# A delta-rule attention feeding an FFN: another layout of the opening, and the input weights' low halves by identity products in PSUM

## The chip, the cores and the metric

One core of one Trainium2 chip. The metric is the device time of one execution in microseconds, median of several runs.

## What is computed

The first part is a linear attention with the delta rule, over 4 batches, 8 heads, 768 positions and a head size of 48. Its output, 3072 tokens of 384 numbers, goes through an FFN with 2048 hidden units:

```python
k_n = k / (np.linalg.norm(k, axis=-1, keepdims=True) + 1e-06)
for t in range(S):
    y[:, :, t] = einsum('bhd,bhde->bhe', q[:, :, t], state)
    v_old = einsum('bhde,bhd->bhe', state, k_n[:, :, t])
    state = state + beta[:, :, t, None] * einsum('bhd,bhe->bhde', k_n[:, :, t], v[:, :, t] - v_old)
x = y.transpose(0, 2, 1, 3).reshape(B * S, H * D)
h = x @ w_in                                    # 384 x 2048
sp = np.maximum(h, 0.0) + np.log1p(np.exp(-np.abs(h)))
out = (h * erf(sp)) @ w_out                     # 2048 x 384
```

q, k, v and beta are f32; the two weight matrices arrive in float64.

## The kernel before

**The attention** is done in 12 chunks of 64 positions; 16 pairs of (batch, head) lie side by side, two heads in the two halves of the partitions. Two chunks make a solve group. For each chunk, TensorE multiplies the keys with themselves (`gram_mm` with "pg", line 259) and the keys with the queries ("pq", the same line); each of these comes in two halves of 16 pairs. `gram_a` (line 269) scales the first on VectorE into A. `gram_p` and `gram_p2` bring the second, masked, into qp, on top of the loaded rows of q. A goes to DRAM and comes back in blocks of 32 (`to_dram`, `to_blocks`); a triangular solve of 31 steps, each a multiply and an add (lines 320 and 322), inverts the blocks in the tile xb, on VectorE for group 0 and on GpSimd for the others; xb goes to DRAM (`put_blocks`, line 327) and from there into xm and A2 (`from_blocks`, `from_blocks2`). The merge (`merge_t` to `merge_m2`: a transposition on VectorE at line 349, products pe, pz and pm at lines 357, 370 and 383) joins the blocks. After it the chain has four steps j per chunk, one per batch: `chain_u`, `chain_s` and `chain_y` (lines 418, 431, 445) with copies between them; step j needs the state that step j - 4 left.

**The FFN** takes four steps j as a group of 256 tokens, 12 groups in all. `x_all` finds the largest magnitude by a product with the identity (`spread`, line 480), `x_tr` transposes, and x is split into two f16 halves xh and xl. The hidden layer has 16 ff tiles of 128 units; two of them make a unit with one PSUM tile ph. `ffn1` (line 622) is nine f16 products per tile: w_in's high half with xh and xl, its low half with xh. `e_sp` (softplus, ScalarE, line 644), `e_erf` (line 649), `e_mul` (line 653, VectorE), `e_split` (a cast to f16, line 660) and `e_rest` (line 666) give two f16 halves of the hidden layer, and `ffn2` (lines 677 to 679) sums their products with w_out in PSUM. Softplus and erf need different tables of ScalarE (line 139).

**The weights** come as pairs of 32-bit words, 12 loads of 512 KB for each matrix (`w_load`, line 490, into raw_in and raw_out). Each load is turned into f32 by `w_mask` (ScalarE, line 496), `w_sign` (VectorE, 503) and `w_bits` twice (VectorE, 509 and 511); `w_sum` (ScalarE, 516) takes the sum of magnitudes. After the last load `w_max`, `w_all` and `w_scale` give one scale per matrix. For each of the 16 ff tiles, `w_hi` (ScalarE, line 550) writes the f16 high half and `w_lo` (VectorE, line 559) the low half, scale x a - h. The f32 tile a lies in the same memory as the halves, one tile further on: the halves of tile i stand where a of tile i - 1 was. The scratch tiles of `early` lie in w_out's memory, so w_out's first loads come late.

**The order** of everything is written by hand. `on(t, fn)` puts down a step with a time; the list is sorted by it and then permuted by the table ORDER (line 33); each engine runs its instructions in that order. `us(x)` turns a time in microseconds into the unit of the table. All DMAs are issued on SyncE's queue, at most eight open at once. `fill` (line 157) puts a dummy matmul on zeros (line 154) on TensorE.

Of the kernel before, what the change touches and what calls it, by code (L numbers as in the profile page):

```python
# [82 lines left out]
@with_exitstack
def delta_ffn_kernel(ctx, tc, kT, qT, ktok, vtok, btok, w_in, w_out, cst, out):
# [151 lines left out]
    def norm_ops(sg, i, w=0):  # L236
        if i == 0:
            no[sg, w] = norms(sg, w)
        for fn in no[sg, w][i:i + 1] if sg < NSP else no[sg, w][3 * i:3 * i + 3]:
            fn()  # L240

    def load_kf(c, name):
        if c == 3 and name == "kpg":
            kf = early(5120, 1024).rearrange("p (a x) -> p a x", a=BP)
        else:
            kf = io.tile([P, BP, C], F32, tag="kf", bufs=3, name=f"{name}{c}")
# [49 lines left out]
    def to_blocks(c):  # L296
        sg, i = divmod(c, 2)
        if i == 0:
            gb_t[sg] = at.tile([P, 32, 32], F32, tag="gb", name=f"gb{sg}") if sg else early(0, 1024).rearrange("p (a b) -> p a b", a=32)
        dv = st[c]["d1"].rearrange("(f s) h a t -> f (h a) s t", f=2)  # L300
        for f in range(2):
            q0 = i * 64 + f * 32
            sp.dma_start(gb_t[sg][q0:q0 + 32], dv[f, :, :, f * 32:f * 32 + 32])

    def solve_init(sg):
        xb_t[sg] = at.tile([P, 32, 32], F32, tag="xb", name=f"xb{sg}") if sg else early(1024, 1024).rearrange("p (a b) -> p a b", a=32)
        x = xb_t[sg].rearrange("p a b -> p (a b)")
        ge.memset(x, 0.0)
        ge.memset(x[:, ::33], 1.0)
# [188 lines left out]
    def w_sign(nm, i):  # L498
        hi = wt[nm]["raw", i][:, :, 1]
        if i in (SGI if nm == "in" else SGO):  # L500
            ge.tensor_scalar(hi, hi.bitcast(F32), 0.0, -2.0 ** 31, op0=ALU.is_lt, op1=ALU.mult)
        else:
            ve.tensor_scalar(hi, hi, -0x80000000, None, op0=ALU.bitwise_and)
# [49 lines left out]

    def w_lo(nm, i, m):
        a, h, l = w_parts(nm, i)
        if m:
# [393 lines left out]
```

## Time and profile before

| | us |
|---|---|
| median of 3 runs | 709.91 |
| lowest and highest | 708.35, 712.67 |
| the profiled execution | 712.84 |
| its span in the trace | 711.1 |

The mean granted clock of TensorE in the profiled execution is 0.966 of 2.4 GHz. All rows further below are from this one execution; times in the trace count from the start of its span. The first product of an FFN group is the mark for how far the attention's opening reaches: group 0 starts at 138.99 us, and everything after it can be read as a second part of the program, in which the chain of the later chunks runs beside the FFN.

### The profile page before, as it was taken

Reading aid. Unit: us, or ns where it says so; the run is one execution under the profiler, and the core shown is the slowest. Engines: PE = TensorE matmul, PEld = TensorE weight load, DVE = VectorE, ACT = ScalarE, POOL = GpSimd, SP = SyncE. Lnnn points to the kernel's source line nnn. Section 1 sums busy time; section 2 is a strip of 40 time slices with the busy share of each in tenths; the row PEclk is TensorE's granted clock in tenths of the full one; section 3 lists DMA queues with packets and bytes.
Section 4 is the critical chain, followed back from the end, with each engine's and each line's share of the span. In section 5 each row is a group of like instructions: output and inputs, shape, how many; then the busy total and the mean of one; then the engine's idle time right before and its main releaser. Section 6 shows DMA issues by size and latency. Waiting matters only on the chain.

```text
span 711.1 us, 22264 instructions
## 1 busy us (share of the span) xinstructions
PE 669.8 (94%) x9475; PEld 507.0 (71%) x9475; DVE 435.9 (61%) x1000; ACT 543.4 (76%) x767; POOL 332.3 (47%) x500
## 2 busy tenths in 40 slices
PE   7999997468999999999999999999999999999997
PEld 5666675356777787886878777877868777777764
DVE  3699859367896874777745659564564455534321
ACT  6214374378899999995994986967978969879993
POOL 4403999344201797898139751178831223201111
PEclk9999997577999999999999999999999999999999
DMA  9486541770004615713445114432041120000000
GB/s 244 105 257 209 166 126 42 210 173 14 3 2 109 152 38 120 159 42 93 85 91 135 35 33 96 101 81 64 18 97 29 26 63 7 24 1 13 12 23 22
DMA packets 87395, 59.05 MB, mean 83 GB/s; under 512 B 67776, under 2 KB 77120, under 8 KB 87296
## 3 DMA queue, kind: packets, MB, share of 16 engines
q1 hardware_dynamic: 87296, 57.63, 32.8%
q8 instruction: 74, 1.21, 0.7%
q14 instruction: 25, 0.20, 0.1%
HBM read 43.45 MB, written 14.16 MB: 81 GB/s over the span
## 4 chain that ended last, share of the span: by engine, by line
PE 67%; ACT 13%; DVE 5%; DMA 5%; issue 4%; POOL 3%; SPq 1%; POOLq 0%; ACTq 0%; DVEq 0%
PE ph L622 18%; PE warm L154 10%; ACT L139 7%; PE pr L677 6%; PE pr L679 6%; PE pr L678 6%; PE pg L259 3%; PE pc L445 3%; PE pc L418 3%; PE pq L259 2%; PE pm L383 2%; DMA k<-ktok 2%; PE pc L431 2%; ACT L L649 2%; ACT L L644 2%
## 5 line engine op out<-in xcount | busy, mean ns | idle before, releaser
L139 ACT ACT_TABLE_LOAD x185 | 237.4, 1283 | 4.0 <-PEq L943 0.7
L622 PE MATMUL ph<-xh,w_in 128*128 128x256 f16 x1152 | 204.2, 274 | 4.2 <-DVE L L653 3.9
L622 PEld LDWEIGHTS <-w_in 128*128 128x128 f16 x1728 | 165.9, 98 | 32.3 <-DVE L L653 4.4
L666 POOL TENSOR_TENSOR H<-L,H 128x512 f16<-128x512 f32 x58 | 67.0, 1157 | 242.9 <-DVE H L662 154.9
L622 PE MATMUL ph<-xl,w_in 128*128 128x256 f16 x576 | 157.4, 273 | 0.0
L653 DVE SCALAR_TENSOR_TENSOR L<-ph,L 128x512 f32<-128x512 f32 x96 | 66.1, 689 | 114.4 <-ACT L L649 107.6
L677 PE MATMUL pr<-w_out,H 128*128 128x384 f16 x384 | 126.0, 328 | 0.0
L679 PE MATMUL pr<-w_out,H 128*128 128x384 f16 x384 | 125.6, 327 | 0.0
L678 PE MATMUL pr<-w_out,H 128*128 128x384 f16 x384 | 125.6, 327 | 0.0
L320 POOL TENSOR_TENSOR tmptmpg<-gb,xb 128x31 f32<-128x31 f32 (+15 forms) x155 | 88.8, 573 | 51.1 <-DMA gb<-d 42.0
L322 POOL TENSOR_TENSOR xb<-xb,tmptmpg 128x31 f32<-128x31 f32 (+15 forms) x155 | 88.6, 571 | 12.1
L644 ACT ACTIVATE L<-ph,xct 128x512 f32<-128x512 f32 x96 | 65.8, 687 | 21.6 <-POOL z L405 9.1
L154 PE MATMUL warm<-zero 128*128 128x384 f16 x455 | 80.2, 337 | 1.1 <-DVE zero L145 1.1
L405 POOL TENSOR_TENSOR z<-v,nm 64x192 f32<-64x192 f32 x96 | 58.5, 609 | 28.8 <-DMA v<-vtok 22.0
L154 PEld LDWEIGHTS <-zero 128*128 128x128 f16 x455 | 44.6, 100 | 31.8 <-issue 3.6
L649 ACT ACTIVATE L<-L 128x512 f32<-128x512 f32 x96 | 60.4, 629 | 1.1
L679 PEld LDWEIGHTS <-H 128*128 128x128 f16 x384 | 37.7, 98 | 25.1 <-issue 0.3
L677 PEld LDWEIGHTS <-H 128*128 128x128 f16 x384 | 37.6, 98 | 20.8 <-issue 0.2
L678 PEld LDWEIGHTS <-H 128*128 128x128 f16 x384 | 37.7, 98 | 18.6 <-issue 0.2
L666 DVE TENSOR_TENSOR H<-L,H 128x512 f16<-128x512 f32 x38 | 28.1, 740 | 25.9 <-ACT H L660 25.8
L424 DVE TENSOR_TENSOR z<-pc,ga 64x192 f32<-64x192 f32 x88 | 31.2, 355 | 17.7 <-PE pc L418 15.3
L259 PE MATMUL pq<-qp,kpq 48*64 48x64 f32 x640 | 25.4, 238 | 16.8 <-DMA qp<-qT 16.8
(138 smaller groups left out, 961.6 us busy)
## 6 DMA issues: line engine op xcount, KB each, us to landing
raw_in<-w_in SPq DMA_DIRECT2D x12, 512.0 KB, 7.6
raw_out<-w_out SPq DMA_DIRECT2D x12, 512.0 KB, 4.8
d<-A SPq DMA_DIRECT2D x20, 256.0 KB, 3.1
k<-ktok SPq DMA_DIRECT2D x12, 384.0 KB, 4.0
qp<-qT SPq DMA_DIRECT2D x24, 192.0 KB, 3.5
v<-vtok SPq DMA_DIRECT2D x48, 96.0 KB, 2.9
out<-ob SPq DMA_DIRECT2D x48, 96.0 KB, 2.2
kpg<-kT SPq DMA_DIRECT2D x22, 192.0 KB, 5.0
```

The source lines that it names most:

```text
L139: se.add_instruction(mybir.InstLoadActFuncSet(name=nc.get_next_instruction_name(), act_func_set_id=i, ins=[], outs=[]))
L154: te.matmul(wp[0], zero[:, :P], zero, start=True, stop=True)
L320: eng.tensor_tensor(tv, G[:, s, s + 1:].unsqueeze(1).broadcast_to([P, ncol, nr]), Xv[:, :, s:s + 1].broadcast_to([P, ncol, nr]), op=ALU.mult)
L322: eng.tensor_tensor(Xv[:, :, s + 1:], Xv[:, :, s + 1:], tv, op=ALU.add)
L622: te.matmul(ph, w[:, i, kt * P:kt * P + P], G[x][:, :, ksl], start=(m == 0), stop=(m == 8))
L644: se.activation(unit(g, u), G["ph", u], AF.Softplus, bias=0.0, scale=G["ct"])
L649: se.activation(Lu, Lu, AF.Erf, bias=0.0, scale=1.0)
L653: ve.scalar_tensor_tensor(Lu, fg[g]["ph", u], HSC, Lu, op0=ALU.mult, op1=ALU.mult)
L666: (ve if u % (2 if g < GLE else GLM) == 0 else ge).tensor_tensor(G["gl", u], unit(g, u), G["gh", u], op=ALU.subtract)
L677: te.matmul(G["po"][a], gh[:, o, asl], wout_h[:, i, :], start=(i == 0), stop=False)
L678: te.matmul(G["po"][a], gh[:, o, asl], wout_l[:, i, :], start=False, stop=False)
L679: te.matmul(G["po"][a], gl[:, o, asl], wout_h[:, i, :], start=False, stop=(i == NFF - 1))
```

## The change

Three things change.

First, the opening has a new layout. w_in's loads 0 to 5 come ahead, w_out's loads get times of their own (WOT), the solves of groups 0 and 1 are moved later in the table, the loads of chunks 2 and 3, of q and of the later kT come later, gram of chunks 2 and 3 is at 63 to 65 us of the table instead of 12 to 16, and v is loaded and scaled earlier for the first six steps. There are 390 fillers, spaced wider, instead of 440. The scratch tiles of `early` for chunk 3, gb and xb of group 0 and A of chunk 3 become tiles of their own. The table ORDER is a new one.

Second, w_in's low halves are made otherwise. TensorE multiplies a with a diagonal of the scale in f32 (`w_lo1`), adds the product of the f16 high half with minus the identity in the same PSUM bank, and ScalarE copies the sum as f16 (`w_lo2`). The banks are pr 0 to 2, in turn. w_out's low halves stay on VectorE.

Third, some steps change engines: for chunks 0 and 1 the mask of pq is multiplied on VectorE straight from PSUM (CP), half of the merge's copies of these chunks (CM) and the state's copy of steps 0 to 3 (S2A) are VectorE's, and the casts of groups 0 and 1 are all ScalarE's (8 more than before).

```diff
-C2 = 2.0
-C3 = 11.5
+C2 = 12.0
+C3 = 16.0
-WU = 440
-MT = 54
+WU = 390
+MT = 58
-WL = (1, 25, 25.1, 25.2, 25.3, 25.4, 25.5, 25.6, 26, 26.1, 26.2, 26.3)
+WL = (0.9, 0.95, 1.0, 1.05, 1.1, 1.15, 24, 24.1, 31.0, 32.5, 34.0, 35.5)
...
-WO = -4.1
+WOT = (36, 38, 40, 42, 76, 78, 62, 86, 88, 90, 72, 74)
+LPE = ("in",)
...
-S2A = (0, 1, 2, 3)
-CP = (0, 1, 2, 3)
-CM = (0,1,2,3)
+S2A = ()
+CP = (2, 3)
+CM = (2, 3)
...
+    def w_ident():
+        ve.tensor_scalar(idn, ident, -1.0, None, op0=ALU.mult)
+
+    def w_idsc(nm):
+        ve.tensor_scalar(ids[nm], ident, wt[nm]["sc"], None, op0=ALU.mult)
+
+    idn = con.tile([P, P], F16, name="idn")
+    ids = {nm: con.tile([P, P], F32, name=f"ids_{nm}") for nm in LPE}
+
+    def w_lo1(nm, i):
+        a, h, _ = w_parts(nm, i)
+        ps = wt[nm]["ps", i] = pr[i % PB][:, :DM]
+        te.matmul(ps, ids[nm], a, start=True, stop=False)
+        te.matmul(ps, idn, h, start=False, stop=True)
+
+    def w_lo2(nm, i):
+        se.copy(w_parts(nm, i)[2], wt[nm]["ps", i])
...
-        if (g * NFF // EU + u) % 8 in SPA:
+        if g < 2 or u in SPA:
             se.copy(G["gh", u], unit(g, u))
...
-    solve_end = [us(42), S1] + [chain_at(2 * sg * B) - MD - 1.3 for sg in range(2, NSG)]
-    solve_start = [us(22), us(30), SS2] + [solve_end[sg - 1] + 1.3 for sg in range(3, NSG)]
+    solve_end = [us(50), us(116)] + [chain_at(2 * sg * B) - MD - 1.3 for sg in range(2, NSG)]
+    solve_start = [us(28), us(76), SS2] + [solve_end[sg - 1] + 1.3 for sg in range(3, NSG)]
...
     for i in range(WU):
-        on(us(6 + 0.12 * i), fill)
+        on(us(6 + 0.17 * i), fill)
...
     for c in range(4):
-        t = (5.5, 8, 12.2, 15)[c]
-        ta = (10.6, 12, 16.3, 18)[c]
+        t = (5.5, 8, 63.2, 65.2)[c]
+        ta = (10.6, 12, 64, 66)[c]
...
-            on(ti, w_hi, nm, i, m)
-            on(ti + 0.2, w_lo, nm, i, m)
+            on(us(76.7 + 0.9 * i) if nm in LPE else ti, w_hi, nm, i, m)
+            if nm in LPE:
+                if i == 0:
+                    on(t + 0.18, w_idsc, nm)
+                tl = us(77 + 0.9 * i)
+                on(tl, w_lo1, nm, i)
+                on(tl + 0.05, w_lo2, nm, i)
+            else:
+                on(ti + 0.2, w_lo, nm, i, m)
```

Three places of the new order. The first is SyncE's queue around the solve of group 1, whose result is written to DRAM at line 327 (323 after the change) from xb into d_2 and d_3. Before, the loads of qp for chunk 2 come behind it:

```order
L398 DMA v_1484<-vtok 128x192
L327 DMA d_2_1684<-xb_163 64x1024
L327 DMA d_3_1694<-xb_163 64x1024
L490 DMA raw_out_1696<-w_out 128x1024
L334 DMA A_2_1700<-d_2_570 32x16x32 x2
L189 DMA qp_0_86<-qT 48x1024
L189 DMA qp_1_87<-qT 48x1024
```

After the change (lines of the new kernel, four less from 189 on):

```order
L245 DMA kpg_1749<-kT 48x1024 x2
L188 DMA qp_0_88<-qT 48x1024
L188 DMA qp_1_89<-qT 48x1024
L290 DMA d_4_2225<-A_2136 64x1024 x2
L323 DMA d_2_2282<-xb_1023 64x1024
L323 DMA d_3_2288<-xb_1023 64x1024
L394 DMA v_2297<-vtok 128x192
L299 DMA gb_2311<-d_4_2225 32x32x32 x2
```

These loads of qp are already those of chunk 3 (qp_0_88 and qp_1_89), which stood 24 rows behind xb's two rows before. Those of chunk 2 (qp_0_86 and qp_1_87) now stand 14 rows further up. So both pairs have moved from behind xb's way to DRAM to ahead of it.

The second is ScalarE around the first input products (softplus at line 644, 655 after; `w_hi` at line 550, 543 after). Before:

```order
L139 ACT_TABLE_LOAD
L644 ACTIVATE L_0_1879<-ph_0_1831,xct_1638 128x512
L550 ACTIVATE w_in<-w_in,sc_in 128x384
L496 ACTIVATE w_out<-raw_out_1799 128x512
L496 ACTIVATE w_out<-raw_out_1803 128x512
L362 COPY T_1841<-pe_1913 32x512 x2
L550 ACTIVATE w_in<-w_in,sc_in 128x384
```

After:

```order
L138 ACT_TABLE_LOAD
L655 ACTIVATE L_0_1789<-ph_0_1759,xct_1487 128x512
L563 CAST w_in<-pr_81 128x384
L543 ACTIVATE w_in<-w_in,sc_in 128x384
L655 ACTIVATE L_0_1789<-ph_1_1793,xct_1487 128x512
L138 ACT_TABLE_LOAD
L509 ACTIVATE raw_out_1541,mx_out<-w_out 128x512
L563 CAST w_in<-pr_82 128x384
L543 ACTIVATE w_in<-w_in,sc_in 128x384
```

Each high half now stands right behind the copy of the low half of the tile before it.

The third is TensorE ahead of the merge (pe at line 357, 353 after). Before, dummies stand on both sides of the first pe:

```order
L154 LDWEIGHTS zero
L154 MATMUL warm<-zero 128x384
L357 MATMUL pe_1083<-T_1067,A_0_656 32x32 x32
L154 LDWEIGHTS zero
L154 MATMUL warm<-zero 128x384
```

After, the last dummy is followed by the half gram of chunk 2, the product that `w_all` needs, and the two pe, and no dummy comes behind them:

```order
L153 LDWEIGHTS zero
L153 MATMUL warm<-zero 128x384
L255 MATMUL pg_1_1052<-kpg_518 64x64 x16
L476 MATMUL spin<-ident,m_in 128x128
L353 MATMUL pe_1088<-T_1073,A_0_546 32x32 x32
L353 MATMUL pe_1134<-w_out 32x32 x32
```

Ahead of the first pe TensorE runs 373 dummies and 12 half grams before, 405 and 10 after; behind it 82 dummies before, none after.

## Rows read from the trace of the kernel before

**Rows 1.** The page: busy times; the chain by line; one group (busy, mean ns).

```profile
PE 669.8 (94%) x9475; PEld 507.0 (71%) x9475; DVE 435.9 (61%) x1000; ACT 543.4 (76%) x767; POOL 332.3 (47%) x500
...
PE ph L622 18%; PE warm L154 10%; ACT L139 7%; PE pr L677 6%; PE pr L679 6%; PE pr L678 6%; PE pg L259 3%; PE pc L445 3%; PE pc L418 3%; PE pq L259 2%; PE pm L383 2%; DMA k<-ktok 2%; PE pc L431 2%; ACT L L649 2%; ACT L L644 2%
...
L139 ACT ACT_TABLE_LOAD x185 | 237.4, 1283 | 4.0 <-PEq L943 0.7
```

**Rows 2.** Chain that ended last, 30 to 140 us: start us, us, what.

```profile
33.54 3.88 PE pg L259 x128
37.42 46.58 PE warm L154 x286
...
126.19 0.45 SPq L327
...
127.38 6.33 DMA raw_out<-w_out
```

**Rows 3.** Waits (total us, times, longest): 110-160; SyncE queue 110-160; TensorE 139-181.

```profile
PE pq L259 <- DMA qp<-qT: 16.8, 3, 10.6
DVE w_in L559 <- ACT w_in L550: 15.0, 5, 10.1
...
SPq L327 <- POOL xb L322: 17.0, 1, 17.0
...
PE pq L259 <- DMA qp<-qT: 6.2, 2, 5.6
```

**Rows 4.** Timeline of SyncE's queue, 105 to 131 us.

```profile
126.19 1.09 SPq L327 DMA_DIRECT2D d<-xb  x2
...
129.72 0.90 SPq L189 DMA_DIRECT2D qp<-qT  x2
```

**Rows 5.** Timeline of TensorE, 125 to 142 us: start us, us, what, idle before it.

```profile
134.94 4.12 PE L259 MATMUL pq<-qp,kpq 48*64 48x64 f32 x64 [10.59 <-DMA qp<-qT]
138.99 0.40 PE L622 MATMUL ph<-xh,w_in 128*128 128x256 f16 x1
```

**Rows 6.** Stretches: busy time of each engine, granted clock, DMA share, GB/s.

```profile
core 0: us, PE busy (x) PEld busy (x) DVE busy (x) ACT busy (x) POOL busy (x), PEclk, DMA share, GB/s
...
117.70:139.00 21.30, 9.16 (x121) 7.65 (x121) 9.76 (x30) 7.04 (x16) 9.22 (x19) 0.50 0.52 134
139.00:162.00 23.00, 15.92 (x338) 14.01 (x339) 16.45 (x30) 17.63 (x33) 12.08 (x14) 0.74 0.73 173
162.00:181.00 19.00, 15.71 (x231) 12.16 (x227) 14.07 (x38) 15.70 (x30) 6.68 (x7) 0.82 0.05 13
181.00:209.00 28.00, 27.72 (x442) 21.64 (x442) 25.41 (x71) 27.16 (x47) 4.88 (x6) 1.00 0.01 2
...
630.00:690.00 60.00, 58.89 (x502) 43.45 (x500) 20.83 (x46) 59.17 (x72) 10.39 (x9) 1.00 0.06 14
```

**Rows 7.** Single lines: duration ns min/median/max, first and last start, forms.

```profile
L269 DVE TENSOR_TENSOR A<-pg,gn x20: 670/682/694, 21.0 to 454.7; 128x512 f32<-128x512 f32 x20
...
L349 DVE STREAM_TRANSPOSE T<-xm x22: 687/701/703, 75.9 to 567.9; 32x512 f32<-32x512 f32 x22
...
L480 PE MATMUL sp<-ident,xm x24: 272/275/376, 116.3 to 656.3; 128*128 128x128 f32 x24
...
L687 ACT ACTIVATE ob<-pr,xco x12: 572/583/588, 235.7 to 705.4; 128x384 f32<-128x384 f32 x12
...
L550 ACT ACTIVATE w_in<-w_in,sc_in x16: 597/612/617, 118.5 to 181.8; 128x384 f16<-128x384 f32 x16
...
L559 DVE SCALAR_TENSOR_TENSOR w_in<-w_in,sc_in x16: 606/619/965, 120.0 to 182.9; 128x384 f16<-128x384 f32 x16
```

**Rows 8.** Stretches of one us around 117, columns as in rows 6.

```profile
115.00:116.00 1.00, 0.70 (x22) 0.55 (x16) 0.97 (x5) 0.82 (x3) 0.92 (x2) 1.00 0.00 0
116.00:117.00 1.00, 0.68 (x4) 0.52 (x4) 1.00 (x3) 0.14 (x1) 0.93 (x3) 1.00 0.00 0
117.00:118.00 1.00, 0.27 (x1) 0.24 (x2) 0.90 (x4) 0.00 (x0) 0.92 (x2) 0.50 0.00 0
```

More of the change, by code (lines that the diff above doesn't have):

```diff
@@ L192, in norm_sq @@
         s = st[c]
-        if c < 4:
+        if c < 2:
             s["sq"] = ff.tile([P, BP, D], F32, tag="L", bufs=LB, name=f"sq{c}")
@@ L238, in norm_ops @@
             no[sg, w] = norms(sg, w)
-        for fn in no[sg, w][i:i + 1] if sg < NSP else no[sg, w][3 * i:3 * i + 3]:
+        for fn in no[sg, w][3 * i:3 * i + 3]:
             fn()
     def load_kf(c, name):
[L243 to L246, printed above, removed]
+        kf = io.tile([P, BP, C], F32, tag="kf", bufs=3, name=f"{name}{c}")
         st[c][name] = kf
@@ L263, in gram_a @@
         if i == 0:
-            if c in (1, 3):
-                s["A"] = early(1024 * (1 + (c + 1) // 2), 1024).rearrange("p (a x) -> p a x", a=BP)
+            if c == 1:
+                s["A"] = early(2048, 1024).rearrange("p (a x) -> p a x", a=BP)
             else:
@@ L298, in to_blocks @@
         if i == 0:
-            gb_t[sg] = at.tile([P, 32, 32], F32, tag="gb", name=f"gb{sg}") if sg else early(0, 1024).rearrange("p (a b) -> p a b", a=32)
+            gb_t[sg] = at.tile([P, 32, 32], F32, tag="gb", name=f"gb{sg}")
         dv = st[c]["d1"].rearrange("(f s) h a t -> f (h a) s t", f=2)
@@ L305, in solve_init @@
     def solve_init(sg):
-        xb_t[sg] = at.tile([P, 32, 32], F32, tag="xb", name=f"xb{sg}") if sg else early(1024, 1024).rearrange("p (a b) -> p a b", a=32)
+        xb_t[sg] = at.tile([P, 32, 32], F32, tag="xb", name=f"xb{sg}")
         x = xb_t[sg].rearrange("p a b -> p (a b)")
@@ L499, in w_sign @@
         hi = wt[nm]["raw", i][:, :, 1]
[L500 to L503, printed above, removed]
+        ve.tensor_scalar(hi, hi, -0x80000000, None, op0=ALU.bitwise_and)
     def w_bits(nm, i, k):
@@ L736, in delta_ffn_kernel @@
     for i in range(WU):
-        on(us(6 + 0.12 * i), fill)
+        on(us(6 + 0.17 * i), fill)
     on(us(0), clear_q)
-    for i, (fn, *a) in enumerate(((load_step, 0), (load_step, 1), (load_beta, 0), (load_kf, 0, "kpg"), (load_kf, 1, "kpg"), (load_q, 0), (load_q, 1),
+    for i, (fn, *a) in enumerate(((load_step, 0), (load_step, 1), (load_beta, 0), (load_kf, 0, "kpg"), (load_kf, 1, "kpg"),
                                   (load_cst,))):
@@ L742, in delta_ffn_kernel @@
     on(us(6.5), clear_x)
+    on(us(19), load_q, 0)
+    on(us(21), load_q, 1)
+    on(us(30), w_ident)
     for sg in range(2):
-        t = (4, 10.5)[sg]
+        t = (4, 20)[sg]
         if sg:
             for i, (fn, a) in enumerate(((load_step, 2), (load_step, 3), (load_beta, 1))):
-                on(us(0.6 + 0.05 * i), fn, a)
+                on(us(14 + 0.05 * i), fn, a)
         for x in range(2):
@@ L763, in delta_ffn_kernel @@
             on(us(ta + 0.6 * i), gram_a, c, i)
-        on(us((11.9, 13.3, 17.6, 19.3)[c]), to_dram, c)
+        on(us((11.9, 13.3, 66, 68)[c]), to_dram, c)
     on(us(14), to_blocks, 0)
@@ L767, in delta_ffn_kernel @@
     on(us(1), solve_init, 0)
-    on(us(0.8), load_kf, 2, "kpg")
-    on(us(0.85), load_kf, 3, "kpg")
+    on(us(30), load_kf, 2, "kpg")
+    on(us(30.5), load_kf, 3, "kpg")
     for c in range(2):
         for i in range(2):
-            t = 20.8 + 2.5 * (2 * c + i)
+            t = (56, 57, 71.5, 73)[2 * c + i]
             on(us(t), gram_mm, c, i, "pq")
-            on(us(t + 2.6), gram_p, c, i)
-            on(us(24.6 + 2.5 * (2 * c + i)), gram_p2, c, i)
+            on(us((64, 65, 72.7, 74.2)[2 * c + i]), gram_p, c, i)
     for sg in range(NSG):
@@ L809, in delta_ffn_kernel @@
             tm = [us(MT + x + 1.25 * c) for x in (0, 1.2, 2.2, 3.6, 4.8, 6, 7.2, 7.3, 8.5)]
-            on(us(22 + c), from_blocks, c)
-            on(us(42.4 + 0.2 * c), from_blocks2, c)
+            on(us(30 + c), from_blocks, c)
+            on(us(50.4 + 0.2 * c), from_blocks2, c)
             if c == 1:
@@ L828, in delta_ffn_kernel @@
         d = 1.0 if j >= 2 * B else 2.6 / SW / CS
-        on(t - 3.3 if j >= 2 * B else t - us(4) + us(0), load_v, j)
-        on(t - 1.2 if j >= 2 * B else t - us(2) + us(0), put_v, j)
+        on(t - 3.3 if j >= 2 * B else us(32 + 2 * j) if j < 6 else t - us(6) + us(0), load_v, j)
+        on(t - 1.2 if j >= 2 * B else us(52 + 1.3 * j) if j < 6 else t - us(2) + us(0), put_v, j)
         on(t, chain_u, j)
@@ L848, in delta_ffn_kernel @@
     for i in range(NRW):
-        t = WO + WD * i
+        t = us(WOT[i])
         on(t - 0.9, w_load, "out", w_out.bitcast(I32), i, RO[i])
@@ L855, in delta_ffn_kernel @@
         on(t + 0.5, w_sum, "out", i)
-    for nm, t in (("in", us(WI[-1] + 3)), ("out", WO + WD * (NRW - 1) + 1.2)):
+    for nm, t in (("in", us(WI[-1] + 3)), ("out", us(max(WOT)) + 1.2)):
         on(t, w_max, nm)
```

12 lines of the change are left out of this document (5 added, 7 removed).

## The prediction

> **What bounds the kernel now.** I read the page first. TensorE is busy 94% of the span, ScalarE 76%, VectorE 61% [rows 1]: a transfer or a VectorE step matters only where TensorE waits for it. A tenth of the chain that ended last is the dummy matmuls of line 154 [rows 1], so the opening is not bound by useful work of TensorE. The chain of waits then says by what. Dummy matmuls stand on it to 84.0 us; from 126.19 it runs through SyncE's queue, and a load of w_out that lands at 133.7 holds ScalarE [rows 2]. So there are two things to look at: where the opening ends, and a hole near 125 us.
>
> The lists of waits give the hole its size. TensorE waited 10.6 us in one piece for qp, VectorE 10.1 us for a high half of w_in, and SyncE stood 17.0 us at line 327 until GpSimd had finished xb [rows 3]. The queue's timeline shows how they hang together: line 327 goes at 126.19, and the loads of qp, which depend on nothing in the solve, stand behind it and go at 129.72 [rows 4]. TensorE starts pq at 134.94 and the first input product of the FFN at 138.99 [rows 5].
>
> The stretches of time give the cost around it. From 117.7 to 139 TensorE is busy 9.16 of 21.3 us, all at the 1.2 GHz level (granted 0.50). In the next two stretches it has 0.74 and 0.82, and is busy 15.92 of 23 and 15.71 of 19. From 181 on it is at 2.4 GHz and nearly full; ScalarE is busy 27.16 of 28 at first, and 59.17 of 60 at the end [rows 6]. What is won before 181 is therefore kept, unless the same stretch costs more elsewhere.
>
> **The end of the opening.** Before, TensorE ran 373 dummy matmuls and 12 half-chunk products of line 259 ahead of the first pe at 84.0. Now it runs 405 and 10. A dummy costs 46.58 / 286 = 0.163 us and a product of 32 matmuls 3.88 / 4 = 0.97 [rows 2]: 32 x 0.163 - 2 x 0.97 = +3.3 us at most, less some idle time in the first 37 us that the new order fills. The last of these products ends at 84 to 87; the mask of it (0.68) and a pair of transposes (1.4) stand behind it on VectorE [rows 7], so pe comes at 86 to 89. I take 87, 3 us late. The solve of group 0 costs nothing here: moved later, it still ends some 10 us ahead of the last dummy.
>
> After pe there were 82 more dummies in the gaps of merge and chain, 13.4 us of TensorE; now there are none. They did not delay what counts, since they filled gaps left by VectorE and GpSimd, and I take the same 33.7 us from pe to the end of the second chunk's chain: 117.7 + 3 = 120.7. The cover that goes with them is the clock's, a rival below. The solve of group 1 starts later too; it ended at 126.19 before and, by its place behind the last gram, may end 30 us later. Its result is wanted by chunk 2, whose tokens are the third group of the FFN, two groups behind the stretch spoken of here: I charge nothing.
>
> **The hole.** In the new queue the loads of qp for chunk 2, and for chunk 3 too, stand ahead of line 323 with xb. TensorE's 10.6 us for qp and VectorE's 10.1 us are gone [rows 3]; the rest of 117.7 to 139, 21.3 - 10.6 = 10.7 us, stays, with pq at 4.1 us [rows 5] if the clock is low and half of that if not. First input product: 120.7 + 10.7 = 131.4. What is late next is w_in's halves, below.
>
> **The low halves.** For 16 ff tiles one VectorE instruction of 0.62 us goes [rows 7], 9.9 us on an engine that is busy 61%: worth nothing by itself. In its place:
> - TensorE: one product of 384 f32 columns and one of 384 f16 columns per tile. The second has a row, 0.163. The first has none. From below it is that of an f16 product, 0.163; from above three f32 products of 128 columns, 3 x 0.275 = 0.83 [rows 7], which is the nearest row in type. Ends 0.33 and 0.99 per tile; I take 0.85, near the upper end, less a little because the records overlap. 16 x 0.85 = 13.6 us, between 5 and 16. Six of them stand ahead of the first input product, in a chain where TensorE has idle time; there I charge 2 of 5.1 us. Ten stand between the input products of the first group, 8.5 us.
> - ScalarE: a copy 128x384 from PSUM, 0.583 by the row of ob, 0.61 by that of the high half [rows 7]. 16 x 0.6 = 9.6 us, of which ten copies, 6.0 us, lie in the first two groups. There, 8 more casts of 0.61 come too (4.9). Against it, three high halves (1.8), two table loads of 1.283 [rows 1] and nine smaller instructions, which I estimate at half a us each, have moved ahead or gone, some 9 us. ScalarE's sum over the two groups grows by about 2 us; since it was idle for 9.5 of those 70 us [rows 6], I charge 1.
> - The hand-off. The halves of tile i overwrite the staging of tile i-1, so ScalarE's next high half waits for TensorE's product, and TensorE for the high half. Each round is 0.61 + 0.85 + 0.6 and some semaphores, 2.1 us, when nothing lies between; ten rounds are 21 us. Before, a round over VectorE was 0.61 + 0.62. From 139 to 181 TensorE stood idle for 10.4 of 42 us and VectorE for 11.5 (busy 16.45 and 14.07) [rows 6]: the ten rounds fit beside the chain in those 42 us, but TensorE's idle time there does not go.
>
> First input product: 131.4 + 2 = 133. From there the kernel took 711.1 - 139.0 = 572 us. Added: 8.5 (low halves) and 1 (ScalarE). Gained: between 139 and 181 TensorE waited for qp a second time, 5.6 us in one piece [rows 3]; that is chunk 3's, now also loaded ahead. Of the 7.0 us that the low clock cost there, 15.92 x 0.26 + 15.71 x 0.18 [rows 6], I credit 2, since the low halves' own products fill some of the gaps. 572 + 9.5 - 7.6 = 574, and the span is 133 + 574 = 707. The profiled execution took 712.84 beside its span of 711.1, and the median of the runs is 709.91, so 707 in the profile is 707 + 1.7 - 2.9 = 706 in the median. That is 0.6% under before; about 1% is what a measurement of this kernel can tell from no change.
>
> Everything else is worth little here: masks of the first chunks on VectorE instead of ScalarE and GpSimd (about 0.7 us each, off the chain), the earlier loads of w_in and v, which take from the same queue as before, and the pieces of staging that no longer live in w_out.
>
> **Rivals.**
> (a) The hand-offs are hidden and the clock stays up: faster by over 1%. pe comes at 86 (1 less), pq runs at 2.4 GHz (2 less) and the first six low halves cost half (1 less): first input product at 129. The other ten are nearer their lower bound (4.5 less), and 3.5 instead of 2 of the 7.0 us come back: the rest takes 568. Span 697, median 696. For it: the queue no longer has the cause of the hole in it. Against it: the granted clock was lost at 117 after two us in which TensorE was busy 70 and 68% [rows 8], with fillers not far ahead of it; the new order has none there.
> (b) The clock falls in the merge and stays down through the hand-offs: slower. Its place is 87 to 165 us. The price: some 10 us of TensorE work of the chain run at half speed, of which half shows (+5), and the six early low halves cost 2 more: first input product at 140. In the ten rounds behind it each low half takes 1.7 instead of 0.85 us, in a loop that ScalarE waits for (+8): the rest takes 582. Span 722, median 721. It decides once more than about 12 us are lost this way. For it: [rows 8], and 82 dummies gone. Against it: the low clock already covers 117 to 139 and parts of 139 to 181 in the kernel before [rows 6], so only the difference counts.
> The Trainium skill, in "TensorE: Matmul & The Clock Gate", section "HAM oscillation — how this bites in real kernels", says that bursts of matmuls with waits between them send the clock down each time, so that a kernel pays for gaps twice. By that rule the hand-off stretch would run at 1.2 GHz from end to end, and the time is that of (b). The trace agrees in part: from 139 to 181, with gaps, the granted clock is 0.74 and 0.82, neither 0.50 nor 1.00.
> (c) The hole only moves: the loads of qp come early, but the solve of group 1, which starts later now, holds the queue at line 323 longer, and TensorE or ScalarE stands there for a load behind it, v or k, for some 9 of the 10.6 us. Then 706 + 9 = 715, within 1%. For it: SyncE stood 17.0 us at that line before [rows 3]. Against it: what the first two groups of the FFN need stands ahead of it in the new queue.
>
> **How the numbers follow.** The forecast and its neighbours get 0.45, (a) 0.25, (b) 0.20, (c) 0.10. The forecast's own range is 700 to 714, and it lies over the 1% line (702.8) with a fifth to a quarter of its chance. Faster by over 1%: 0.25 + 0.10 = 0.35. Slower by over 1% (716.9): all of (b) and a little of (c), 0.22. Within 1%: 0.43. The range for 8 in 10 runs from the middle of (a), 694, to (b), 721.
>
> **What would show it.** Right: no wait of TensorE for qp over 3 us before the first input product; that product at 131 to 135; VectorE no longer among the waits of w_in; ScalarE waiting for the products of lines 559 and 560 in rounds of about 2 us; the f32 product at 0.6 to 0.83 us of TensorE; from the first product to the end 571 to 577. Wrong: granted clock 0.50 ahead of 115 (then b), pe later than 90, a product of line 559 above 1 us, or a new hole of over 5 us in which the queue of SyncE waits.

## The result, and the profile after

The changed kernel takes 705.08 us in the median of 20 runs (701.94 to 714.99), the kernel before 712.25 us in 20 runs of the same job (707.75 to 715.39). The ratio is 0.9907, with a 95% interval of 0.9886 to 0.9929: faster by 0.9%, some 6.6 us. The slowest of the 20, 714.99, fell in a slower state and is left out of the ratio. The profiled execution took 704.88 us beside a span of 703.1.

First the page of the changed kernel: the busy times and the chain by line.

```profile
PE 672.3 (96%) x9473; PEld 508.2 (72%) x9473; DVE 443.3 (63%) x1000; ACT 543.6 (77%) x767; POOL 310.1 (44%) x492
...
PE ph L633 18%; PE warm L153 9%; ACT L138 8%; PE pr L688 7%; PE pr L690 6%; PE pr L689 6%; PE pg L255 3%; PE pc L441 3%; ACT L L660 3%; PE pq L255 3%; ACT L L655 2%; PE pc L414 2%; PE pc L427 2%; DVE z L435 2%; PE pm L379 1%
```

TensorE is busy 672.3 us, 2.5 more than in [rows 1], in a span 8.0 us shorter, so it stands idle 10.5 us less. The dummies' share of the chain is 9%, after 10%.

Where the time went is read best by marks on TensorE. One row of the kernel before that was not needed so far is its first output product (line 677):

```profile
175.58 0.50 PE L677 MATMUL pr<-w_out,H 128*128 128x384 f16 x1
```

And TensorE's timeline of the changed kernel (start us, us, what, and in brackets the idle time before it and what ended it): the first pe, the first low half (lines 559 and 560), the first input product (633), a low half at full clock with what follows it, and the first output product (688).

```profile
86.58 1.20 PE L353 MATMUL pe<-T,A 32*32 32x32 f32 x64 [1.17 <-DVE m_in L521]
...
112.95 1.65 PE L559 MATMUL pr<-w_in,ids_in 128*128 128x384 f32 x2 [0.81 <-ACT y L450]
114.39 0.53 PE L560 MATMUL pr<-w_in,idn 128*128 128x384 f16 x1
...
133.34 0.27 PE L633 MATMUL ph<-xh,w_in 128*128 128x256 f16 x1
...
144.99 0.81 PE L559 MATMUL pr<-w_in,ids_in 128*128 128x384 f32 x2
...
145.80 0.27 PE L633 MATMUL ph<-xh,w_in 128*128 128x256 f16 x1
...
167.63 0.34 PE L688 MATMUL pr<-w_out,H 128*128 128x384 f16 x1
```

| mark | before | after | difference |
|---|---|---|---|
| first pe (line 357, now 353) | 84.00 | 86.58 | +2.6 |
| first input product | 138.99 | 133.34 | -5.7 |
| first output product | 175.58 | 167.63 | -8.0 |
| end of the span | 711.1 | 703.1 | -8.0 |

From the first output product to the end both kernels take 535.5 us. So the whole gain lies ahead of it, between the merge and the end of the FFN's first units. The stretches there (columns as in [rows 6]):

```profile
83.00:95.00 12.00, 5.29 (x184) 4.71 (x185) 10.37 (x21) 3.63 (x8) 0.00 (x0) 0.72 0.72 194
95.00:100.00 5.00, 5.00 (x150) 4.82 (x146) 4.92 (x10) 2.22 (x6) 0.00 (x0) 0.50 0.01 3
...
110.00:117.00 7.00, 5.68 (x81) 3.94 (x83) 5.12 (x14) 1.87 (x4) 1.90 (x6) 0.65 1.01 193
117.00:128.00 11.00, 9.57 (x108) 6.21 (x104) 7.46 (x22) 7.86 (x20) 8.43 (x17) 0.76 1.05 315
128.00:133.30 5.30, 5.30 (x102) 4.06 (x103) 4.15 (x12) 4.86 (x11) 3.13 (x3) 1.00 0.51 113
133.30:148.00 14.70, 12.66 (x135) 9.53 (x133) 12.71 (x24) 14.59 (x29) 13.53 (x17) 1.00 0.17 50
148.00:162.00 14.00, 10.19 (x110) 7.03 (x109) 13.22 (x35) 13.38 (x27) 12.67 (x20) 1.00 0.01 2
...
167.60:181.00 13.40, 13.40 (x127) 9.84 (x124) 8.12 (x11) 13.26 (x19) 12.23 (x18) 1.00 0.61 136
```

From 128 us on the granted clock is 1.00, where the kernel before had 0.50, 0.74 and 0.82 between 117 and 181 [rows 6]. Ahead of it there are low stretches: 0.72 between 83 and 95, 0.50 from 95 to 100, 0.65 and 0.76 between 110 and 128. ScalarE is busy 14.59 of 14.7 and 13.38 of 14 us behind the first input product, and GpSimd 13.53 and 12.67: the solve of group 1, which ended at 126 before, runs here now. The waits of TensorE from 84 to 200 us (us in total, times, longest):

```profile
PE pe L353 <- DVE T L358: 3.3, 1, 3.3
...
PE pq L255 <- DMA qp<-qT: 1.1, 1, 1.1
```

The wait of 10.6 us for qp [rows 3] has shrunk to 1.1.

### The profile page after: what moved, and what is told of

It is laid out like the page before. It is cut to its first block, busy times and chain, and to the rows that moved or that the text cites. A ratio compares the mean times of both kernels' runs of the same rounds, so it can differ in the third digit from the quotient of the medians.

```text
span 703.1 us, 22214 instructions
## 1 busy us (share of the span) xinstructions
PE 672.3 (96%) x9473; PEld 508.2 (72%) x9473; DVE 443.3 (63%) x1000; ACT 543.6 (77%) x767; POOL 310.1 (44%) x492
## 4 chain that ended last, share of the span: by engine, by line
PE 65%; ACT 19%; DVE 8%; issue 3%; DMA 3%; SPq 0%; POOL 0%; ACTq 0%; POOLq 0%
PE ph L633 18%; PE warm L153 9%; ACT L138 8%; PE pr L688 7%; PE pr L690 6%; PE pr L689 6%; PE pg L255 3%; PE pc L441 3%; ACT L L660 3%; PE pq L255 3%; ACT L L655 2%; PE pc L414 2%; PE pc L427 2%; DVE z L435 2%; PE pm L379 1%
## 5 line engine op out<-in xcount | busy, mean ns | idle before, releaser
L633 PE MATMUL ph<-xh,w_in 128*128 128x256 f16 x1152 | 216.6, 273 | 4.2 <-DVE L L664 4.2
L401 POOL TENSOR_TENSOR z<-v,nm 64x192 f32<-64x192 f32 x96 | 51.5, 536 | 100.1 <-DMA v<-vtok 59.5
L316 POOL TENSOR_TENSOR tmptmpg<-gb,xb 128x31 f32<-128x31 f32 (+15 forms) x155 | 83.5, 539 | 25.1 <-DMA gb<-d 16.1
L153 PE MATMUL warm<-zero 128*128 128x384 f16 x405 | 70.2, 337 | 1.1 <-DVE zero L144 1.1
L153 PEld LDWEIGHTS <-zero 128*128 128x128 f16 x405 | 40.4, 101 | 29.3 <-issue 3.7
L671 ACT CAST H<-L 128x512 f16<-128x512 f32 x56 | 34.3, 614 | 18.2 <-DVE L L664 17.9
L435 DVE TENSOR_TENSOR z<-pc,z 48x192 f32<-48x192 f32 x80 | 28.2, 353 | 26.6 <-PE pc L441 26.0
```

Source lines behind the costliest of these rows:

```text
L153: te.matmul(wp[0], zero[:, :P], zero, start=True, stop=True)
L316: eng.tensor_tensor(tv, G[:, s, s + 1:].unsqueeze(1).broadcast_to([P, ncol, nr]), Xv[:, :, s:s + 1].broadcast_to([P, ncol, nr]), op=ALU.mult)
L633: te.matmul(ph, w[:, i, kt * P:kt * P + P], G[x][:, :, ksl], start=(m == 0), stop=(m == 8))
```

## The experiments

All ratios are to runs of the kernel before on the same chip in the same job, with the 95% interval. The intervals are some 0.4 to 0.8% wide in all, so differences below 2 to 3 us between two experiments are not told apart. The marks and rows of an experiment are those of one execution.

**The two parts, each alone.** First the new layout without the new low halves: the changed kernel with VectorE's old instruction at the place of the copy. The third part of the change, the steps that change engines, stays with the layout here and below; no run parts the two.

```diff
     def w_lo1(nm, i):
...
-        te.matmul(ps, ids[nm], a, start=True, stop=False)
-        te.matmul(ps, idn, h, start=False, stop=True)

     def w_lo2(nm, i):
-        se.copy(w_parts(nm, i)[2], wt[nm]["ps", i])
+        a, h, l = w_parts(nm, i)
+        ve.scalar_tensor_tensor(l, a, wt[nm]["sc"], h, op0=ALU.mult, op1=ALU.subtract)
```

> The changed kernel with w_in's low halves back on VectorE, one instruction at the place of the copy; no products for them on TensorE. Theory 1 (the low halves' new form costs a little, since ScalarE sets the pace behind the first input product): 1 to 4 us faster than the changed kernel, ratio to before 0.985 to 0.990. Theory 2 (freeing VectorE is the gain): slower than the changed kernel by 4 us or more, ratio 0.996 or above, with VectorE full and waited for between 133 and 168 us.

Measured: 1.0006 (0.9985 to 1.0027). The new layout, with those steps, gives nothing alone, and the low halves' new form is worth 1.0% on top of it. My theory 1 fell here. The stretches of this run:

```profile
117.00:128.00 11.00, 7.69 (x116) 6.35 (x118) 10.48 (x28) 7.47 (x17) 9.26 (x16) 0.57 1.06 308
...
133.00:148.00 15.00, 9.69 (x106) 7.83 (x104) 14.68 (x24) 11.63 (x21) 13.83 (x17) 0.70 0.10 28
148.00:162.00 14.00, 7.59 (x99) 6.59 (x98) 13.41 (x35) 8.85 (x17) 10.69 (x15) 0.74 0.01 1
```

Its first input product comes at 131.3, 2 us earlier than in the changed kernel, but the first output product only at 172.5, 4.9 later. VectorE is full between 133 and 148 (14.68 of 15). TensorE's clock is low too (0.57 to 0.74). So there were two candidates, VectorE and the clock.

Then the new low halves without the new layout: the kernel before, with the products and the copy at the place of VectorE's instruction (one bank, pr 2, for all tiles).

```diff
     def w_lo(nm, i, m):
         a, h, l = w_parts(nm, i)
+        if nm == "in":
+            if i == 0:
+                ve.tensor_scalar(idn, ident, -1.0, None, op0=ALU.mult)
+                ve.tensor_scalar(ids, ident, wt[nm]["sc"], None, op0=ALU.mult)
+            te.matmul(pr[2][:, :DM], ids, a, start=True, stop=False)
+            te.matmul(pr[2][:, :DM], idn, h, start=False, stop=True)
+            se.copy(l, pr[2][:, :DM])
+            return
```

> The kernel before, in its old layout, with w_in's low halves formed by the two products and a copy by ScalarE, at the place in the order where VectorE formed them. VectorE was not full there (16.45 of 23 us and 14.07 of 19), and GpSimd's solve was over by 126. By theory 3 the new form wins nothing by itself: ratio 0.998 to 1.008, the upper part if the copy holds up ScalarE's queue. If the new form is the gain by itself: 0.990 to 0.994.

Measured: 1.0082 (1.0053 to 1.0111), the upper end of what theory 3 (below) expected. The new form alone loses 0.8%. The waits of this run from 117 to 181 us point to the reason: ScalarE's copy stands in its queue for the product.

```profile
ACT w_in L565 <- PE pr L564: 18.3, 9, 4.8
```

In the changed order the product is issued a little earlier and other work of ScalarE lies between. With one bank in place of three this run is a little harder on the new form than the change is.

**Clock or VectorE?** The products stay on TensorE, their sum unused, and VectorE forms the low halves.

```diff
     def w_lo2(nm, i):
-        se.copy(w_parts(nm, i)[2], wt[nm]["ps", i])
+        a, h, l = w_parts(nm, i)
+        ve.scalar_tensor_tensor(l, a, wt[nm]["sc"], h, op0=ALU.mult, op1=ALU.subtract)
```

> The changed kernel with w_in's low halves formed on VectorE, as in the run before that lost 7 us, but with the two products of every low half left on TensorE, their sum unused. If that run lost its time because TensorE stood idle there and its clock fell to 1.2 GHz (granted 0.57 to 0.74 between 117 and 162), the products keep the clock up and most of the loss is gone: ratio to before 0.990 to 0.994. If it lost it because VectorE is full (14.68 of 15 us) and the high halves wait for it, the loss stays: 0.999 to 1.004.

Measured: 1.0022 (0.9992 to 1.0052). The loss stays, although TensorE now has the work, and the clock is higher:

```profile
133.00:148.00 15.00, 10.92 (x106) 7.24 (x105) 14.68 (x24) 11.47 (x21) 13.75 (x18) 0.90 0.11 28
148.00:162.00 14.00, 9.72 (x86) 6.93 (x85) 13.41 (x34) 8.82 (x17) 10.67 (x15) 0.99 0.01 1
```

The clock is 0.90 and 0.99 instead of 0.70 and 0.74, and VectorE is as full as in the run before. So a higher clock did not bring the time back. The products left on TensorE may have cost some time themselves (done twice, further below, they cost some 6 us), so that the clock is worth little here is shown only together with the run without the solve below. Half of the tiles each way:

```diff
     def w_lo1(nm, i):
+        if i % 2:
+            return
...
     def w_lo2(nm, i):
-        se.copy(w_parts(nm, i)[2], wt[nm]["ps", i])
+        if i % 2:
+            a, h, l = w_parts(nm, i)
+            ve.scalar_tensor_tensor(l, a, wt[nm]["sc"], h, op0=ALU.mult, op1=ALU.subtract)
+        else:
+            se.copy(w_parts(nm, i)[2], wt[nm]["ps", i])
```

> The changed kernel with the low halves of the odd ff tiles on VectorE, without products and copy, and those of the even tiles as they are. If VectorE and ScalarE are each the bound when all 16 are theirs, half and half is under both: as fast as the changed kernel or up to 3 us faster (ratio to before 0.986 to 0.991). If the clock decides, TensorE has 6.5 us less to do in that stretch and the clock falls: 2 to 5 us slower than the changed kernel (0.993 to 0.998).

Measured: 0.9987 (0.9955 to 1.0018). No optimum in between: eight of VectorE's instructions cost most of what sixteen did. That is outside both ranges and nearer to the clock's, so the expectation from VectorE, that half and half lies under both bounds, was wrong. The trace shows that VectorE can be the bound all the same:

```profile
133.00:148.00 15.00, 11.76 (x118) 8.39 (x116) 14.67 (x26) 13.37 (x25) 13.98 (x15) 0.89 0.14 37
```

With half of the low halves VectorE is still busy 14.67 of 15 us, against 12.71 of 14.7 in the changed kernel. The clock is lower too (0.89), so this run does not decide between the two.

**Why VectorE is full.** Theory 3: the layout laid the solve of group 1 beside the low halves, and VectorE's instructions take longer while GpSimd runs. In the run with the new layout and all low halves on VectorE, its groups between 117 and 168 us read (busy us, mean ns, idle before), and the wait of ScalarE for the low halves from 100 to 181 (us in total, times, longest):

```profile
L562 DVE SCALAR_TENSOR_TENSOR w_in<-w_in,sc_in 128x384 f16<-128x384 f32 x13 | 10.9, 835 | 0.0
L620 DVE SCALAR_TENSOR_TENSOR xl<-pt,xsx,xh 64x128 f16<-64x128 f32 (+1 forms) x12 | 4.3, 385 | 0.1
L504 DVE SCALAR_TENSOR_TENSOR w_out<-raw_out,w_out 128x512 int32<-128x512 int32 x4 | 4.1, 1023 | 0.1
L496 DVE TENSOR_SCALAR raw_out<-raw_out 128x512 int32<-128x512 int32 x4 | 2.5, 620 | 0.0
...
ACT w_in L543 <- DVE w_in L562: 10.7, 11, 2.7
```

The low half takes 835 ns in the mean (0.55 to 1.62 us over all 16), and a step of `w_bits` 1023, against 0.62 for the low half in [rows 7] and 0.69 for the same step of `w_bits` in the changed kernel's opening, where GpSimd's solve does not run. The experiment takes the solve away. It leaves out the inversion of group 1's blocks, so its outputs from chunk 2 on are others.

```diff
     def solve_row(sg, s, eng, tag, j0=0, j1=32):
+        if sg == 1:
+            return
         G = gb_t[sg]
```

> The run with the low halves on VectorE in the new layout, now without the 31 steps of group 1's solve on GpSimd (left out: the inversion of group 1's blocks, so the outputs from chunk 2 on are others). Theory 3: the new layout laid that solve beside the low halves, and VectorE's instructions take longer while GpSimd runs (0.97 to 1.6 us instead of 0.61). Then without the solve they take 0.6 to 0.7, VectorE is no longer full, and the time falls to ratio 0.984 to 0.992. If VectorE simply has too many instructions there, the time stays: 0.997 to 1.002.

Measured: 0.9896 (0.9863 to 0.9929), 1.1% less than with the solve. VectorE's groups and ScalarE's wait as above, and the stretches:

```profile
L564 DVE SCALAR_TENSOR_TENSOR w_in<-w_in,sc_in 128x384 f16<-128x384 f32 x15 | 11.0, 733 | 1.5 <-ACT w_in L545 1.5
L622 DVE SCALAR_TENSOR_TENSOR xl<-pt,xsx,xh 64x128 f16<-64x128 f32 (+1 forms) x12 | 4.3, 387 | 0.1
L506 DVE SCALAR_TENSOR_TENSOR w_out<-raw_out,w_out 128x512 int32<-128x512 int32 x5 | 3.5, 694 | 0.1
L504 DVE SCALAR_TENSOR_TENSOR w_out<-w_out,raw_out 128x512 int32<-128x512 int32 x4 | 2.9, 737 | 0.1
L498 DVE TENSOR_SCALAR raw_out<-raw_out 128x512 int32<-128x512 int32 x4 | 1.7, 423 | 0.0
...
ACT w_in L545 <- DVE w_in L564: 5.5, 5, 2.2
```

```profile
133.00:148.00 15.00, 11.09 (x117) 9.03 (x115) 12.64 (x27) 11.95 (x22) 1.84 (x2) 0.74 0.17 43
148.00:162.00 14.00, 7.57 (x101) 6.57 (x99) 12.48 (x42) 11.61 (x20) 1.16 (x1) 0.73 0.01 1
```

`w_bits` is back at 694 and 737 ns, the low half at 733, and VectorE is busy 12.64 of 15 us. ScalarE waits 5.5 us for the low halves instead of 10.7. And the clock is as low as in the run that lost (0.74 and 0.73), so a low clock alone does not cost the time here. The mean of 733 hides two kinds of low half. GpSimd still has the mask of qp to do from 129.10 to 134.92, and the low half that starts beside it takes 1.61 us, the next one, with GpSimd idle, 0.61:

```profile
129.10 5.82 POOL L283 TENSOR_TENSOR qp<-qp,mask 64x512 f32<-64x512 f32 x4 [8.17 <-ACT qp L274]
...
133.72 1.61 DVE L564 SCALAR_TENSOR_TENSOR w_in<-w_in,sc_in 128x384 f16<-128x384 f32 x1
...
137.04 0.61 DVE L564 SCALAR_TENSOR_TENSOR w_in<-w_in,sc_in 128x384 f16<-128x384 f32 x1
```

The control is the changed kernel without the same solve:

> Control: the changed kernel without the 31 steps of group 1's solve (the same part left out). By theory 3 VectorE was not full here, so little is won: ratio to before 0.985 to 0.990, at most 4 us under the changed kernel, and at most 2 us faster or slower than the run before with the low halves on VectorE: without the solve both ways of forming them cost about the same.

Measured: 0.9888 (0.9849 to 0.9926). That is within the interval of the changed kernel and of the run above. Without the solve both ways of forming the low halves cost the same; with it, VectorE's costs 1.0% more. The Trainium skill, in "GPSIMD Engine Reference", section "1. Specifications", says that GpSimd shares its SBUF interfaces with VectorE and that VectorE's instructions contend with it when they have two SBUF inputs or run in a 2-port mode. The traces agree on the first: the low half and `w_bits` have two inputs in SBUF and stretch from 0.62 to 0.84 and from 0.69 to 1.02 us, while `xl`, one of whose inputs lies in PSUM, takes 385 ns with the solve and 387 without. `w_sign`, with one input, stretches too (620 ns against 423); whether it runs in a 2-port mode no run here shows. One limit remains: the run takes away GpSimd's time in its own queue together with its accesses, so the size of the two is not separated. The control speaks for the accesses: there the same time is gone from the queue, and 0.2% is won, inside the interval.

| | low halves on VectorE | on TensorE and ScalarE |
|---|---|---|
| old layout | 1 | 1.0082 |
| new layout | 1.0006 | 0.9907 |
| new layout, without group 1's solve | 0.9896 | 0.9888 |

**Which engine sets the pace now.** Each half of the new form was done twice; the second time overwrites the first.

```diff
-        te.matmul(ps, ids[nm], a, start=True, stop=False)
-        te.matmul(ps, idn, h, start=False, stop=True)
+        for _ in range(2):
+            te.matmul(ps, ids[nm], a, start=True, stop=False)
+            te.matmul(ps, idn, h, start=False, stop=True)
```

> The changed kernel with the two products of every low half done twice (the second overwrites the first): 16 x 0.81 = 13 us more of TensorE. If ScalarE sets the pace from 128 to 168 us, most of it goes into idle time there: 3 to 7 us more than the changed kernel (ratio to before 0.995 to 1.001). If TensorE sets it, all of it shows: 12 to 14 us more (1.008 to 1.011).

Measured: 0.9994 (0.9971 to 1.0016), 0.9% above the changed kernel: some 6 of 13 us show, give or take 2.

```diff
-        se.copy(w_parts(nm, i)[2], wt[nm]["ps", i])
+        for _ in range(2):
+            se.copy(w_parts(nm, i)[2], wt[nm]["ps", i])
```

> The changed kernel with the copy of every low half done twice on ScalarE: 16 x 0.47 = 7.5 us more of ScalarE, 4.7 of them behind the first input product. If ScalarE sets the pace there, 4 to 7 us more than the changed kernel (ratio to before 0.996 to 1.001). If TensorE sets it, under 2 us more (0.990 to 0.993).

Measured: 0.9987 (0.9960 to 1.0014): some 6 of 7.5 us show, give or take 2. So a microsecond more of ScalarE costs most of itself and one of TensorE about half. Not all of it lies behind the first input product: in the two profiled executions that product comes at 136.7 and 137.0, over 3 us later than in the changed kernel. Product and copy both stand between two of ScalarE's high halves, so the load of the engines and the length of that loop are not told apart here.

**The queue alone.** The kernel before with the loads of w_out number 8 and of qp for chunk 2 ahead of xb's way to DRAM. For this and the runs below each step in the list carries its name and numbers.

```diff
         ev = [ev[i] for i in ORDER]
+    pos = lambda *k: next(i for i, e in enumerate(ev) if e[3][:len(k)] == k)
+    w8 = next(i for i, e in enumerate(ev) if e[3][0] == "w_load" and e[3][1] == "out" and e[3][3] == 8)
+    for k in (w8, pos("load_q", 2)):
+        ev.insert(pos("put_blocks", 2), ev.pop(k))
```

> The kernel before with one thing changed: the loads of qp for chunk 2 and of w_out number 8 stand ahead of xb's way to DRAM in SyncE's queue. Theory 1 (the change's gain is the hole in that queue): the 10.6 us wait of TensorE for qp is gone or under 3 us, the first input product comes at 129 to 132 instead of 139, and the time is 6 to 10 us under before (ratio 0.986 to 0.992), as much as the whole change gave. Theory 2 (the gain is VectorE freed of the low halves, or the layout as a whole): the wait only moves, the first input product stays after 136, ratio 0.996 to 1.002.

Measured: 0.9948 (0.9929 to 0.9967), between the two theories. The first input product comes at 127.2, 11.8 us earlier than before and earlier than I expected, but only a third of it arrives at the end. The next waits, in the timelines of ScalarE and TensorE:

```profile
135.00 0.67 ACT L496 ACTIVATE w_out<-raw_out 128x512 f32<-128x512 f32 x1 [6.44 <-DMA raw_out<-w_out]
...
150.87 0.45 PE L259 MATMUL pq<-qp,kpq 48*64 48x64 f32 x2 [6.25 <-DMA qp<-qT]
```

ScalarE stands 6.44 us for the next load of w_out, behind which the high halves wait, and TensorE 6.25 us for the qp of chunk 3. The second FFN unit pair starts at 157.5, against 162.2 before. The hole had moved on, as rival (c) feared, though to other loads than v or k. The new layout, which has w_out's loads and both pairs of qp out of that stretch, closes it, and gains nothing by that alone, as the run with VectorE's low halves showed.

**The clock in the merge.** 43 dummies in the gaps where the clock fell.

```diff
+    for n, k in ((20, ("merge_e", 0)), (10, ("merge_e", 1)), (8, ("chain_u", 3)), (5, ("chain_u", 4))):
+        i = pos(*k) + 1
+        ev[i:i] = [(0, 0, fill, ("fill",))] * n
```

> The changed kernel with 43 dummy matmuls more: 20 behind the first pe, 10 behind the second, 8 behind the first product of chain step 3 and 5 behind that of step 4, where TensorE is idle and the clock falls (0.50 from 88 to 101 and from 112 to 122). If the low clock there is paid on the path, the chain between 91 and 123 runs 3 to 5 us shorter and the time is 2 to 5 us under the changed kernel (ratio to before 0.984 to 0.988). If the path there is VectorE's and the loads', no change within 1.5 us (0.989 to 0.993); if the dummies stand in the way, slower by 1 to 3.

Measured: 0.9890 (0.9860 to 0.9921), median 703.29 us. The stretches of this run:

```profile
95.00:110.00 15.00, 13.43 (x431) 11.87 (x430) 13.19 (x27) 6.37 (x14) 0.00 (x0) 1.00 0.22 55
110.00:117.00 7.00, 6.85 (x113) 4.61 (x112) 5.87 (x16) 2.26 (x5) 1.65 (x3) 1.00 0.85 191
117.00:128.00 11.00, 8.42 (x131) 5.68 (x129) 10.11 (x27) 9.17 (x22) 9.62 (x19) 1.00 1.05 337
```

From 95 on the clock is 1.00 (between 110 and 117 it was 0.65), and the first input product comes at 130.8 in this execution, 2.5 us earlier. The ratio is 0.2% under the changed kernel's and inside its interval, so a gain of 1 to 2 us is likely from the trace and not shown by the times. Then 20 of the dummies ahead of the last half gram of chunk 2 taken away as well:

```diff
+    first = pos("merge_e", 0)
+    drop = [i for i, e in enumerate(ev) if e[3][0] == "fill" and i < first][-20:]
+    ev = [e for i, e in enumerate(ev) if i not in drop]
```

> The changed kernel with the 43 dummies in the merge and 20 dummies fewer ahead of the last half gram of chunk 2. If that gram, for which VectorE waited 3.0 us, is the end of the opening, pe comes 2 to 3 us earlier and the time is 1 to 3 us under the run with the 43 dummies (ratio to before 0.984 to 0.988). If the loads of xm are, which go out from 76.9 to 81.4 us, nothing more is won: 0.988 to 0.990.

Measured: 0.9891 (0.9856 to 0.9925), median 705.12 us. No further gain is shown. Its profiled execution had the first input product at 127.5 and was the fastest of its six, 699.16 us; the slowest took 706.76. Whether it is better than the run above stays open.

**A miss.** The second half of chunk 0's mask moved behind the merge's copies on VectorE.

```diff
+    e = ev.pop(pos("gram_p", 0, 1))
+    ev.insert(pos("chain_u", 0), e)
```

> The changed kernel with the second half of chunk 0's mask (two VectorE instructions, 1.4 us) moved from between the transposes and the copies of the merge to behind these copies. If VectorE's queue is the path there (TensorE waited 3.3 us for T of the second chunk), the merge ends 1 to 1.4 us earlier and the time follows by 0.5 to 1.5 us (ratio to before 0.988 to 0.990). If not, no change.

Measured: 0.9947 (0.9921 to 0.9972). Slower than the changed kernel by 0.4%, if anything, where I expected a small gain; the intervals overlap. In its trace the first input product comes at 134.4, 1 us later. I did not look for the cause further.

## Why the prediction was right, and where it was not

The time came out as forecast, 705.1 for 706, 0.9% under before where 0.6% was said, and inside "within 1%". The mark of the first input product held. Behind it two errors of 11 and 15 us cancelled, so that the number is this close is luck. (Two slips of the prediction weigh nothing: 1% over 709.91 is 717.0, not 716.9, and the middle of (a) is 696 by its own sum, not 694.)

**The end of the opening**: held. pe was said at 87, measured 86.58.

**From pe to the first input product**: held, 46.8 us for 46. The clock fell where rival (b) put it, from 88 and from 112, and two of the signs of being wrong came up: a clock of 0.50 ahead of 115 (from 95 to 100), and 1.65 us for the first product of line 559. But that delayed the product little. The run with the dummies shows some 2.5 us in one execution. The sum held better than its steps: in the chain that ended last, VectorE's steps fill most of 84 to 94 us, and from 116.25 to 127.98 stand two loads that the prediction did not have on the path:

```profile
116.25 7.29 DMA raw_out<-w_out
...
123.56 4.42 DMA A<-d
```

**The hole**: held for its place. The wait for qp went from 10.6 to 1.1 us. But the layout's worth was mis-stated. By my steps the layout alone, without the low halves, would have ended the span near 698 (first product at 131.4, from there 572 - 5.6 and little more). The run that has just this had its first product at 131.3, as worked out, and a span of 708.4: 577 from there, 11 us more. The step that failed is "I charge nothing" for the solve of group 1. I asked who waits for its result, and not what it runs beside. Laid beside the FFN's first units, it stretched VectorE's instructions until VectorE was full. The trace of the kernel before had the sign of it, in the opening, where that solve ran then: the same step of `w_bits` takes 0.68 us before GpSimd starts the solve at 64.28 and 1.10 beside it.

```profile
62.10 0.68 DVE L509 SCALAR_TENSOR_TENSOR w_in<-w_in,raw_in 128x512 int32<-128x512 int32 x1
...
78.14 1.10 DVE L509 SCALAR_TENSOR_TENSOR w_in<-w_in,raw_in 128x512 int32<-128x512 int32 x1
```

**The low halves**: "worth nothing by itself" for the relief of VectorE was wrong, for the same reason. I took VectorE's share of the span, 61%, and its idle time between 139 and 181 in the old layout, where GpSimd's solve had ended. In the new layout the relief is worth 1.0% with its price paid, where I had charged some 9 us for the price alone. The pieces of the price were near: a product pair takes 0.81 us from start to start at full clock (0.85 taken). The copy on ScalarE takes 0.47, where 0.6 was taken. The hand-offs did not come in ten rounds of waiting: ScalarE stood for the product of line 560 twice, 3.9 us in all.

```profile
L563 ACT CAST w_in<-pr x16: 457/470/483, 115.0 to 165.6; 128x384 f16<-128x384 f32 x16
```

**From the first input product to the end**: 574 was said, 569.8 measured. The sum is made of two errors. Without the low halves' new form it should have been 572 - 5.6 = 566.4, and was 577.1, 10.7 more. The new form was to add 9.5 - 2 = 7.5, and took 7.3 off, 14.8 less than said. The clock's term, 2 of 7.0 us credited, cannot be judged by itself: the granted clock was 1.00 throughout, but the run without the solve had 0.74 and 0.73 and lost nothing that the intervals show. That ScalarE would be full there was not said for this stretch: I charged 1 us for it, and the doubled copy shows that a microsecond more of ScalarE costs about 0.8.

**The rivals**: (a) came nearest in mechanism behind the first product, since the clock stayed up there and little waiting was left in the hand-offs, as (b) did ahead of it, at little cost. By the rule of the Trainium skill as it was read with (b), the stretch with hand-offs would have run at 1.2 GHz; it ran at 2.4 GHz. But the case that the Trainium skill describes there, in "TensorE: Matmul & The Clock Gate", section "HAM oscillation — how this bites in real kernels", has bursts of products shorter than the waits between them. Here TensorE was busy 12.66 of 14.7 us and 10.19 of 14, so the rule was applied to another case. A hole that moves, as in (c), is what the queue's edit alone shows.

## What to carry to other kernels

When a step is moved, ask what it will run beside, not only who waits for its result: the solve on GpSimd was harmless by its due time, and made VectorE's larger two-input instructions beside it longer by up to half in the mean (0.69 to 1.02 us). An engine's share of the span, and its idle time in the old order, say nothing about the relief it needs in the new one; the price list of a stretch has to be made for the engines as they will stand there. And parts of a change can be worth nothing or less apart and 1% together, so each should be tried with and without the other before it is judged.

## What the runs showed of the hardware

The stretching beside GpSimd is, for its length, largest where the instructions are smallest, in the few that the traces have. VectorE's groups on 128x32 elements between 117 and 168 us, in the changed kernel:

```profile
L222 DVE SCALAR_TENSOR_TENSOR ri<-t,ri 128x32 f32<-128x32 f32 x3 | 1.7, 550 | 0.1
...
L217 DVE TENSOR_SCALAR ri<-n 128x32 int32<-128x32 int32 x1 | 1.1, 1080 | 0.0
...
L225 DVE RECIPROCAL ri<-nm 128x32 f32<-128x32 f32 x1 | 0.4, 353 | 0.0
```

and without the solve:

```profile
L222 DVE SCALAR_TENSOR_TENSOR ri<-t,ri 128x32 f32<-128x32 f32 x3 | 0.6, 192 | 0.1
...
L225 DVE RECIPROCAL ri<-nm 128x32 f32<-128x32 f32 x1 | 0.4, 353 | 0.0
...
L217 DVE TENSOR_SCALAR ri<-n 128x32 int32<-128x32 int32 x1 | 0.2, 181 | 0.0
```

Lines 222 and 217 go from 192 and 181 ns to 550 (three instructions) and 1080 (one), although they move 32 elements per partition; the reciprocal takes 353 in both. So the wait is not in proportion to the work, and not every kind of instruction has it.

The clock and the time came apart twice: low clock without loss (the run without the solve, 0.74 and 0.73), and high clock with the loss kept (products left on TensorE, 0.90 and 0.99). So in these stretches the granted clock does not tell what holds the path.
